# Moving three small parameter loads and their transpose behind other work, in a one-core SSM + SwiGLU kernel

## The chip, the core and the metric

The kernel runs on one core of a Trainium2 chip. The core has four compute engines with queues of their own: TensorE (PE in the profile; PEld is its weight load), VectorE (DVE), ScalarE (ACT) and GpSimd (POOL). SyncE (SP) only issues transfers. Each engine takes its instructions in the order of its queue, and engines wait for each other by semaphores. Transfers can be issued from SyncE's, ScalarE's and GpSimd's queue; all of them are carried out by the core's 16 DMA engines. Matrix products land in PSUM, which has eight banks; everything else lies in SBUF.

The metric is device time in microseconds (us), the median over several executions. A profile is one further execution, with every instruction's start and duration. Its times count from the first instruction, so its span is a little shorter than the device time of the same execution.

## The reference

The input x has 2048 tokens of 512 features. It is normalised, and then two branches run on the result and are added to x: an S5 state-space layer (A) and a SwiGLU feed-forward layer (B).

```
xn = layernorm(x)
# A: S5, state size 512, complex
dt = exp(log_dt);  Lam = Lambda_re + 1j * Lambda_im
Lam_bar = exp(dt * Lam)
Bu = xn @ (((Lam_bar - 1) / Lam)[:, None] * (B_re + 1j * B_im)).T
h[t] = Lam_bar * h[t - 1] + Bu[t]
y = 2 * Re(h @ C.T) + xn * Dskip
# B: SwiGLU, hidden size 1376
ffn = (silu(xn @ w_gate) * (xn @ w_up)) @ w_down
out = x + y + ffn
```

The change concerns the three vectors Lambda_re, Lambda_im and log_dt, of 512 bf16 numbers (1 KB) each.

## The kernel before

The 2048 tokens are cut into 16 token tiles of 128, and these into 4 chunks of 512. For chunks 1 to 3 the normalised tokens are transposed by DMA, and gate, up, B's projection and the output products run on the transposed chunk. The first chunk is treated in another way, so that TensorE has work before all of x and all statistics are there: token tiles 0 to 3 are transposed on TensorE (`raw_mm`, `cT_mm`, line 244), their mean is taken off, and gate and up of each tile are multiplied with the centred tile (`head_mm`, `sw_mm`, line 488) while the factor 1/std is applied when the products are read out of PSUM (`sw_out`, lines 497 and 498). Weights of gate and up come in three groups (`wg0`, `wu0`; `wg1`, `wu1`; `w_end`).

The order of each engine's queue is the order of the program text: the schedule is written by hand (`tc.manual_schedule()`), and the tail of the function is that order. Later work on VectorE is queued in a backlog and let out by an estimate of TensorE's time (`pump`, `need`).

What bears on the change:

- **The parameter vectors.** `prm_rows` is a tile of 128 by 128, set to zero on GpSimd (line 141). Three loads on GpSimd's queue (line 143) put each vector into four of its rows. These stand near the beginning of GpSimd's queue. `prm_transpose` (lines 278 to 281) transposes the tile on TensorE into bank `p1` (line 280), and VectorE copies the 12 useful columns to `prm` (line 281). TensorE's weight load for it waits for all three loads.
- **dt and what follows.** `exp_pool` raises e to the power on GpSimd (line 284): `dt_t` from `prm`, later `r_t`. `params_a` (lines 287 to 289) and `params_sin` (lines 325 to 341) follow on VectorE and ScalarE; ScalarE's two sines stand between its `sw_out` of token tile 1 and that of token tile 2. The tables (line 300 and on) take `ws2` and `jidx`.
- **Around it on GpSimd.** Four powers for 1/std of token tiles 1, 0, 3 and 2 (line 197); `pad_last` (lines 510 and 512) and an iota for `jidx` (line 725).
- **Around it on VectorE.** The copies of the transposed token tile 1 (line 256), statistics (lines 187 to 196), centring (line 234), and `norm_dve` (line 205), which normalises token tiles 0 to 3 for the DMA transpose of chunk 0 (`xT_dma(0)`, line 264, SyncE's queue).
- **PSUM.** Eight banks are handed round in the order in which they come free; a matmul into a bank waits for the last reader of what was there.
- **SyncE's queue at that time** issues, in this order: the second group of gate and up, `w_end` for gate and up (line 114), token tiles 4 to 7 of x (line 144), the DMA transpose of B_re (line 148), and then `xT_dma(0)`.

In the order written by hand, the stretch around the transpose is:

```
    head_mm(0, 2)
    for k in range(KD):
        cT_mm(p0, xc[:, 3, :], k, k == 0, k == KD - 1)
    cT_copy(nc.scalar.copy, p0, 3)
    prm_transpose()
    exp_pool(dt_t[:], ldt)
    pad_last()
```

Of the kernel before, what the change touches and what calls it, by code (L numbers as in the profile page):

```python
# [23 lines left out]
def kernel(  # L24
# [17 lines left out]
    nc = tc.nc  # L42
# [10 lines left out]
    NQ = Pst // 128  # L53
# [20 lines left out]
    def bank(shape=(128, CW), dtype=F32):  # L74
        return psum.tile(list(shape), dtype, name="ps")
# [62 lines left out]
    load_w1(nc.sync, wg_g, wg_v, 2)  # L138
    load_w1(nc.sync, wu_g, wu_v, 2)
    prm_rows = const.tile([128, 128], BF16, name="prm_rows")  # L140
    nc.gpsimd.memset(prm_rows[:], 0.0)
    for i, v in enumerate((A_Lambda_re, A_Lambda_im, A_log_dt)):
        nc.gpsimd.dma_start(out=prm_rows[i * NQ:(i + 1) * NQ, :], in_=v.rearrange("(q j) -> q j", j=128))
    nc.sync.dma_start(out=xall[:, TPC:2 * TPC, :], in_=x_v[:, TPC:2 * TPC, :])

    def load_bt(part):
# [31 lines left out]
    def xn_tile(c):  # L178
        if c not in xn_c:
            xn_c[c] = lnp.tile([128, KD, TPC, 128], BF16, name="xn")  # L180
        return xn_c[c]

    def by_k(ap):
        return ap.rearrange("p (k d) -> p k d", d=128)

    def ln_stats(n):
        nc.vector.bn_stats(out=stats[:, n, 0, :], in_=xall[:, n, :])  # L187
        nc.vector.bn_aggr(out=mv[:, n, :], in_=stats[:, n, 0, :])
# [14 lines left out]
    def norm_dve(n):  # L203
        c, i = divmod(n, TPC)
        nc.vector.tensor_scalar(out=xn_tile(c)[:, :, i, :], in0=by_k(xall[:, n, :]), scalar1=mv[:, n, 0:1],
                                scalar2=rstd[:, n:n + 1], op0=ALU.subtract, op1=ALU.mult)
# [19 lines left out]
    def mean_act(i):  # L226
        nc.scalar.activation(out=xnT[:, NCH - 1, 0, :], in_=xall[:, i, :], func=ACT.Copy, scale=1.0 / D,
                             accum_out=mean2[:])
# [26 lines left out]
    def cT_copy(copy, ps, i, k0=0, k1=KD):  # L255
        copy(out=xcT[:, k0:k1, i * 128:(i + 1) * 128], in_=by_k(ps[:, k0 * 128:k1 * 128]))  # L256
# [6 lines left out]
    def xT_dma(c):  # L263
        nc.sync.dma_start_transpose(out=runs(xnT[:, c]), in_=xn_tile(c)[:].rearrange("p k i d -> p (k i d)"))

    prm = const.tile([128, 3, NQ], F32, name="prm")
    lre, lim, ldt = prm[:, 0, :], prm[:, 1, :], prm[:, 2, :]

    def sm(name, *shape):
        return const.tile([128, *shape], F32, name=name)  # L270

    dt_t, r_t, dre = sm("dt_t", NQ), sm("r_t", NQ), sm("dre", NQ)
# [5 lines left out]
    def prm_transpose():  # L278
        pp = p1[:, 0:128]
        nc.tensor.matmul(pp, lhsT=prm_rows[:], rhs=ident[:], start=True, stop=True)  # L280
        V.tensor_copy(out=prm[:].rearrange("p t q -> p (t q)"), in_=pp[:, 0:3 * NQ])

    def exp_pool(out, in_):
        nc.gpsimd.tensor_tensor(out=out, in0=e_t[:], in1=in_, op=ALU.pow)
# [200 lines left out]
    def sw_mm(ps, groups, gi, i, k0=0, k1=KD):  # L485
        a, b = fgroups[gi]
        for k in range(k0, k1):
            nc.tensor.matmul(ps[:, 0:(b - a) * 128], lhsT=xcT[:, k, i * 128:(i + 1) * 128], rhs=groups[gi][:, k, 0:(b - a) * 128],  # L488
                             start=(k == 0), stop=(k == KD - 1))
# [19 lines left out]
    def pad_last():  # L509
        nc.gpsimd.memset(g0[:, FT - 1, :, FR:128], 0.0)  # L510
        for t in g_last:
            nc.gpsimd.memset(t[:, :, FR:128], 0.0)
# [157 lines left out]
    def head_mm(which, i, k0=0, k1=KD):  # L670
        if held[i][which] is None:
            held[i][which] = bank()
        sw_mm(held[i][which], (G, U)[which], 0, i, k0, k1)
# [22 lines left out]
    for k in range(HK, KD):  # L696
        for i in range(2):
            head_mm(0, i, k, k + 1)
    ln_stats(1)
    mean_act(2)  # L700
    ln_rstd(1, 2)
# [17 lines left out]
    for k in range(KD):  # L719
        cT_mm(p0, xc[:, 3, :], k, k == 0, k == KD - 1)  # L720
    cT_copy(nc.scalar.copy, p0, 3)
    prm_transpose()
    exp_pool(dt_t[:], ldt)
    pad_last()
    nc.gpsimd.iota(out=jidx[:], pattern=[[1, CW]], base=0, channel_multiplier=0,
                   allow_small_or_imprecise_dtypes=True)
    sw_out(0, 0, *held[0])
    head_mm(1, 2)
    for n in range(TPC):
        norm_dve(n)  # L730
    xT_dma(0)
    params_a()
# [146 lines left out]
```

## Time and profile before

| | us |
|---|---|
| median of 3 runs (lowest, highest) | 178.70 (178.49, 178.71) |
| the profiled execution's own time | 178.46 |
| its span, first to last instruction | 176.4 |
| TensorE busy | 172.9 (98% of the span) |
| VectorE busy | 158.1 (90%) |
| ScalarE busy | 106.6 (60%) |
| GpSimd busy | 27.8 (16%) |

The granted TensorE clock is 0.999. The page's rows of busy tenths cut the span into 40 slices of 4.4 us each; the DMA row gives the mean busy share of the 16 DMA engines:

```profile
PE   8999999999999999999999999999999999999993
DVE  3899999999999999999999999999999997799133
POOL 5272300050000000047000000024100002416100
DMA  6999839999996000037015000007410000993712
```

A 9 is 90% or more. TensorE is busy from the first slice to the last but one. VectorE has hardly a gap until slice 33. GpSimd works little, most of it in the first slices. The DMA engines are filled in slices 1 to 3 (4 to 18 us), where x, the weights and B's matrices come in.

In the profile's lists, a line of the timeline gives start, duration, engine, program line, operation, output <- inputs, and count; square brackets give the idle time before it and what ended it. "us to landing" is the time from the issue of a transfer to its completion. A group such as "x4" is four instructions in a row; matmuls overlap, so a group's duration is a little longer than the distance to the next one's start.

### The profile page before, as it was taken

The numbers are of one execution on the slowest core, as the hardware profiler recorded it, in microseconds if no ns is written. First come the engines' busy times: TensorE is split into PE (matmuls) and PEld (weight loads), VectorE is DVE, ScalarE is ACT, GpSimd is POOL, SyncE is SP. The second block draws the span as 40 slices with busy tenths as digits, with TensorE's granted clock in tenths as the row PEclk, the third lists the DMA queues.
The fourth block names the chain that finished last, engine by engine and source line by source line (L and its number), as shares of the span: only waits on it lengthen the run. The fifth ranks groups of instructions, "written<-read, shape, count | busy, mean of one in ns | idle before, by whom it ended". The sixth has DMA issues, their size and how long they took to land.

```text
span 176.4 us, 2469 instructions
## 1 busy us (share of the span) xinstructions
PE 172.9 (98%) x904; PEld 85.4 (48%) x904; DVE 158.1 (90%) x261; ACT 106.6 (60%) x192; POOL 27.8 (16%) x39
## 2 busy tenths in 40 slices
PE   8999999999999999999999999999999999999993
PEld 4444755564444444446444444446444444444743
DVE  3899999999999999999999999999999997799133
ACT  4468989978976687036896661024666657962000
POOL 5272300050000000047000000024100002416100
PEclk9999999999999999999999999999999999999999
DMA  6999839999996000037015000007410000993712
GB/s 169 340 351 203 177 88 250 224 169 337 238 238 238 4 0 0 0 33 85 16 20 119 0 0 0 0 4 71 48 30 2 4 0 0 160 181 48 90 44 75
DMA packets 35179, 17.88 MB, mean 101 GB/s; under 512 B 25008, under 2 KB 35088, under 8 KB 35120
## 3 DMA queue, kind: packets, MB, share of 16 engines
q1 hardware_dynamic: 30992, 13.96, 33.8%
q0 software_dynamic: 3456, 3.28, 14.6%
q10 hardware_dynamic: 720, 0.49, 0.9%
q8 instruction: 7, 0.11, 0.3%
q14 instruction: 4, 0.03, 0.1%
HBM read 8.03 MB, written 5.24 MB: 75 GB/s over the span
## 4 chain that ended last, share of the span: by engine, by line
PE 97%; DMA 1%; DVE 0%; issue 0%
PE ps L461 29%; PE ps L579 22%; PE ps L589 16%; PE ps L386 16%; PE ps L488 10%; PE ps L521 3%; DMA xall<-in_A_x_dram 1%; PE ps L244 1%; PE ps L252 0%; DVE xall L592 0%; PE ps L646 0%; PE ps L280 0%
## 5 line engine op out<-in xcount | busy, mean ns | idle before, releaser
L579 PE MATMUL ps<-wd_sb,guT 128*128 128x512 bf16 (+3 forms) x198 | 38.8, 355 | 0.0
L428 DVE TENSOR_TENSOR_SCAN g<-r_t,car,u 128x512 bf16<-128x512 f32 x24 | 29.1, 1264 | 0.0
L589 PE MATMUL ps<-CF,wt 128*128 128x512 bf16 (+2 forms) x144 | 28.3, 355 | 0.0
L386 PE MATMUL ps<-xnT,BT 128*128 128x512 bf16 x128 | 28.3, 379 | 0.0
L579 PEld LDWEIGHTS <-guT 128*128 128x128 bf16 (+1 forms) x198 | 18.5, 98 | 19.9
L461 PE MATMUL ps<-xnT,wg 128*128 128x512 bf16 x96 | 24.6, 379 | 0.0
L461 PE MATMUL ps<-xnT,wu 128*128 128x512 bf16 x96 | 24.6, 379 | 0.0
L596 POOL DMA_DIRECT2D out_dram<-res x12 | 10.5, 1043 | 81.6 <-ACT res L595 76.0
L595 ACT CAST res<-ps 128x512 bf16<-128x512 f32 x12 | 7.0, 584 | 24.7 <-PE ps L589 24.7
L388 ACT CAST u<-ps 128x512 bf16<-128x512 f32 x32 | 18.2, 590 | 5.9 <-PE ps L386 5.8
L475 ACT ACTIVATE guT<-ps 128x512 bf16<-128x512 f32 x30 | 17.9, 596 | 6.1 <-PE ps L461 6.1
L476 ACT CAST u<-ps 128x512 bf16<-128x512 f32 x30 | 17.6, 587 | 6.0 <-PE ps L461 6.0
L589 PEld LDWEIGHTS <-wt 128*128 128x128 bf16 x144 | 13.4, 98 | 14.3
L386 PEld LDWEIGHTS <-BT 128*128 128x128 bf16 x128 | 12.5, 98 | 14.7
L551 ACT ACTIVATE xr<-xall,nb,rstd 128x512 bf16<-128x512 bf16 x16 | 11.8, 804 | 5.2 <-DVE xall L559 3.0
L461 PEld LDWEIGHTS <-wu 128*128 128x128 bf16 x96 | 9.4, 98 | 11.3
L461 PEld LDWEIGHTS <-wg 128*128 128x128 bf16 x96 | 9.4, 98 | 10.6
L488 PEld LDWEIGHTS <-CF 128*128 128x128 bf16 x96 | 9.1, 98 | 8.0 <-ACT CF L256 0.8
L197 POOL TENSOR_TENSOR rstd<-ve,neg_half 128x1 f32<-128x1 f32 (+1 forms) x7 | 7.6, 1084 | 26.7 <-DVE ve L196 26.7
L461 PE MATMUL ps<-xnT,w_end 128*128 128x512 bf16 x48 | 10.8, 379 | 0.0
L187 DVE BATCH_NORM_STATS2 stats<-xall 128x6 f32<-128x512 bf16 x15 | 10.1, 674 | 0.2 <-DMA xall<-in_A_x_dram 0.2
L480 DVE TENSOR_TENSOR guT<-guT,u 128x1024 bf16<-128x1024 bf16 x15 | 10.0, 675 | 0.0
(120 smaller groups left out, 217.9 us busy)
## 6 DMA issues: line engine op xcount, KB each, us to landing
out_dram<-in_A_x_dram SPq DMA_DIRECT2D x3, 512.0 KB, 5.2
out_dram<-res POOLq DMA_DIRECT2D x12, 128.0 KB, 3.1
out_dram<-xall POOLq DMA_DIRECT2D x3, 512.0 KB, 6.1
wd_sb<-in_B_w_down_dram SPq DMA_DIRECT2D x1, 1280.0 KB, 7.2
xall<-in_A_x_dram SPq DMA_DIRECT2D x1, 1024.0 KB, 7.3
wu<-in_B_w_up_dram SPq DMA_DIRECT2D x2, 256.0 KB, 4.4
wg<-in_B_w_gate_dram SPq DMA_DIRECT2D x1, 512.0 KB, 5.3
wu<-in_B_w_up_dram SPq DMA_DIRECT2D x1, 512.0 KB, 5.4
```

The source lines that it names most:

```text
L187: nc.vector.bn_stats(out=stats[:, n, 0, :], in_=xall[:, n, :])
L386: nc.tensor.matmul(ps[:], lhsT=BT[:, part, k, q * 128:(q + 1) * 128], rhs=xnT[:, c, k, :], start=(k == 0), stop=(k == KD - 1))
L388: nc.scalar.copy(out=u_tiles[c][:, part, q, :], in_=ps[:])
L428: V.tensor_tensor_scan(out=g()[:, part, q, :], data0=r_t[:, q:q + 1].to_broadcast([128, CW]), data1=u_tiles[c][:, part, q, :], initial=ini ...
L461: nc.tensor.matmul(ps[:fs, lo:hi], lhsT=wslice(groups, fi, k), rhs=xnT[:, c, k, lo:hi], start=(k == 0), stop=(k == KD - 1))
L475: nc.scalar.activation(out=guT[:fs, fi, :], in_=psg[:fs], func=ACT.Silu)
L476: nc.scalar.copy(out=u_pair[c][:fs, fi % 2, :], in_=psu[:fs])
L488: nc.tensor.matmul(ps[:, 0:(b - a) * 128], lhsT=xcT[:, k, i * 128:(i + 1) * 128], rhs=groups[gi][:, k, 0:(b - a) * 128], start=(k == 0), s ...
L551: nc.scalar.activation(out=box["xr"][:], in_=xall[:, n, :], func=ACT.Identity, scale=rstd[:, n:n + 1], bias=nb[:, n:n + 1])
L579: nc.tensor.matmul(o[:], lhsT=gu_tiles[c][:fsz[fi], fi, i * 128:(i + 1) * 128], rhs=wd_sb[:fsz[fi], fi, lo:hi], start=(fi == 0), stop=False)
L589: nc.tensor.matmul(o[:], lhsT=w_tiles[c][:, part, q, i * 128:(i + 1) * 128], rhs=CF[:, part, q, lo:hi], start=False, stop=(part == 1 and q ...
L596: nc.gpsimd.dma_start(out=out_v[:, n, lo:hi], in_=res[:, lo:hi], accum_op=ALU.add)
```

## The change

The memset of `prm_rows` and its three loads become a function, `load_prm`, called behind the copies of token tile 1 instead of near the start. The memset is done by VectorE instead of GpSimd; the loads stay on GpSimd's queue. The transpose and the power for `dt` move from behind the copy of token tile 3 into the loop that normalises token tiles 0 to 3, ahead of the third of them.

```
@@ -138,9 +138,12 @@
     prm_rows = const.tile([128, 128], BF16, name="prm_rows")
-    nc.gpsimd.memset(prm_rows[:], 0.0)
-    for i, v in enumerate((A_Lambda_re, A_Lambda_im, A_log_dt)):
-        nc.gpsimd.dma_start(out=prm_rows[i * NQ:(i + 1) * NQ, :], in_=v.rearrange("(q j) -> q j", j=128))
+
+    def load_prm():
+        nc.vector.memset(prm_rows[:], 0.0)
+        for i, v in enumerate((A_Lambda_re, A_Lambda_im, A_log_dt)):
+            nc.gpsimd.dma_start(out=prm_rows[i * NQ:(i + 1) * NQ, :], in_=v.rearrange("(q j) -> q j", j=128))
+
@@ -696,6 +699,7 @@
     for k in range(HK, KD):
         for i in range(2):
             head_mm(0, i, k, k + 1)
+    load_prm()
     ln_stats(1)
     mean_act(2)
@@ -719,14 +723,15 @@
     cT_copy(nc.scalar.copy, p0, 3)
-    prm_transpose()
-    exp_pool(dt_t[:], ldt)
     pad_last()
     nc.gpsimd.iota(out=jidx[:], pattern=[[1, CW]], base=0, channel_multiplier=0,
                    allow_small_or_imprecise_dtypes=True)
     sw_out(0, 0, *held[0])
     head_mm(1, 2)
     for n in range(TPC):
+        if n == 2:
+            prm_transpose()
+            exp_pool(dt_t[:], ldt)
         norm_dve(n)
     xT_dma(0)
```

In the built program this gives, queue by queue: on TensorE the transpose stands behind the four matmuls of up of token tile 2 and ahead of gate of token tile 3; on VectorE the memset stands between the copy of token tile 1 and its statistics, and the copy of `prm` between the second and the third `norm_dve`; on GpSimd the three issues stand ahead of the four powers for 1/std, and the power for `dt` behind `pad_last` and the iota. The number of instructions is the same. SyncE's and ScalarE's queues keep their order. Since `p1` now comes free later, banks are handed round a little differently: up of token tile 3 takes the bank that held gate of token tile 0, and the first matmul group with the second group of weights takes `p1`.

More of the change, by code (lines that the diff above doesn't have):

```diff
@@ L140, with load_prm @@
     prm_rows = const.tile([128, 128], BF16, name="prm_rows")
-    nc.gpsimd.memset(prm_rows[:], 0.0)
-    for i, v in enumerate((A_Lambda_re, A_Lambda_im, A_log_dt)):
-        nc.gpsimd.dma_start(out=prm_rows[i * NQ:(i + 1) * NQ, :], in_=v.rearrange("(q j) -> q j", j=128))
+    def load_prm():
+        nc.vector.memset(prm_rows[:], 0.0)
+        for i, v in enumerate((A_Lambda_re, A_Lambda_im, A_log_dt)):
+            nc.gpsimd.dma_start(out=prm_rows[i * NQ:(i + 1) * NQ, :], in_=v.rearrange("(q j) -> q j", j=128))
     nc.sync.dma_start(out=xall[:, TPC:2 * TPC, :], in_=x_v[:, TPC:2 * TPC, :])
@@ L698 @@
             head_mm(0, i, k, k + 1)
+    load_prm()
     ln_stats(1)
@@ L721 @@
     cT_copy(nc.scalar.copy, p0, 3)
-    prm_transpose()
-    exp_pool(dt_t[:], ldt)
     pad_last()
@@ L729 @@
     for n in range(TPC):
+        if n == 2:
+            prm_transpose()
+            exp_pool(dt_t[:], ldt)
         norm_dve(n)
```

## The prediction

> **What bounds the kernel now.** I read the chain of work that ended last first, then TensorE's waits, then the order of time on each engine around the moved lines, and last the transfers in flight there. The page's chain line and the one wait that TensorE has:
>
> ```profile
> PE 97%; DMA 1%; DVE 0%; issue 0%
> ```
> ```profile
> PE ps L646 <- PEq L863: 0.8, 1, 0.8
> ```
>
> After its first instruction TensorE (PE) waits for nobody that the profile shows until its last matmul at 173.7. So whatever holds its queue up is added to the time one for one, and nothing gets faster by being relieved elsewhere. A speeded-up VectorE or ScalarE is worth nothing here. TensorE around the transpose (start, duration, line):
>
> ```profile
> 9.79 0.39 PE L244 MATMUL ps<-ident,CF 128*128 128x128 bf16 x4
> 10.01 0.22 PE L280 MATMUL ps<-ident,prm_rows 128*128 128x128 bf16 x1
> 10.07 1.03 PE L488 MATMUL ps<-wu,CF 128*128 128x512 bf16 x4
> 10.93 1.03 PE L488 MATMUL ps<-wg,CF 128*128 128x512 bf16 x4
> ```
>
> L280 takes a slot of 0.06 (10.07 - 10.01). Behind the four matmuls of up of token tile 2 it would start at 10.93 - 0.06 = 10.87. That is the due time of the parameter rows after the change, against 10.01 before: 0.86 later. GpSimd (POOL) before:
>
> ```profile
> 1.78 0.71 POOL L143 DMA_DIRECT2D prm_rows<-in_A_Lambda_re_dram  x1 [0.31 <-POOL prm_rows L141]
> 2.48 0.56 POOL L143 DMA_DIRECT2D prm_rows<-in_A_Lambda_im_dram  x1
> 3.03 0.52 POOL L143 DMA_DIRECT2D prm_rows<-in_A_log_dt_dram  x1
> ...
> 11.26 1.02 POOL L284 TENSOR_TENSOR dt_t<-e_t,prm 128x4 f32<-128x4 f32 x1
> 12.23 0.20 POOL L510 MEMSET guT<- 128x128 bf16 x1
> ```
>
> The third load is issued at 3.03. What the reader is to see next is how long a load is under way while the weights fill the DMA engines (issues in narrow windows: size, us from issue to landing):
>
> ```profile
> xall<-in_A_x_dram SPq DMA_DIRECT2D x1, 128.0 KB, 4.3
> prm_rows<-in_A_Lambda_im_dram POOLq DMA_DIRECT2D x1, 1.0 KB, 3.9
> wu<-in_B_w_up_dram SPq DMA_DIRECT2D x1, 256.0 KB, 4.3
> prm_rows<-in_A_log_dt_dram POOLq DMA_DIRECT2D x1, 1.0 KB, 4.1
> ```
> ```profile
> w_end<-in_B_w_gate_dram SPq DMA_DIRECT2D x1, 352.0 KB, 5.6
> w_end<-in_B_w_up_dram SPq DMA_DIRECT2D x1, 352.0 KB, 6.2
> xall<-in_A_x_dram SPq DMA_DIRECT2D x1, 512.0 KB, 7.0
> ```
> ```profile
> dsk_bc<-in_A_Dskip_dram POOLq DMA_DIRECT2D x1, 128.0 KB, 5.8
> wd_sb<-in_B_w_down_dram SPq DMA_DIRECT2D x1, 96.0 KB, 7.2
> ```
>
> With the issue times of the SyncE and GpSimd timelines: xall tile 2 (2.13) lands at 6.4, Lambda_im (2.48) at 6.4; wu's first half (2.60) at 6.9, log_dt (3.03) at 7.1. A load of 1 KB on GpSimd's queue lands together with the large transfer that SyncE issued just before it. Much later it is the same: dsk_bc (38.63) lands at 44.4, the 96 KB of wd_sb issued at 37.33 at 44.5. So the small loads stand behind the backlog that is there when they are issued, and that backlog grows: w_end gate, issued at 6.44, lands at 12.0; w_end up (6.86) at 13.1; xall tiles 4 to 7 (7.52) at 14.5.
>
> **The change part by part.**
>
> *Memset.* GpSimd's memset of 0.21 goes; VectorE does one of the same tile, behind the copies of token tile 1. Nearest rows: 0.17 for minus_mean's memset of the same size, 0.06 for one of four columns. I take 0.1 to 0.17. VectorE comes to it at about 5.5 (L187 starts at 5.52 before). The 0.33 that it idles before L234 at 7.27 takes this up. Without that idle, 0.15 would reach the copy of token tile 2 and TensorE's four L244 behind it.
>
> *The three issues.* GpSimd waits for the memset (done at about 5.65) and then starts the first issue 0.3 later, as at L143 before (0.31 idle): 5.95. With the spacings of before (0.70 and 0.55) the others start at 6.65 and 7.2, the last ends at 7.72. Queued behind them on GpSimd is the power for rstd of tile 1 (6.69 before, now about 7.75 to 8.35). Its readers are ScalarE at 11.85 and VectorE at 11.1, and the next one on GpSimd waits for VectorE until 8.47 anyway: nothing on the path. SyncE's queue is not touched. The 96 small packets leave the window of 4 to 7 us; the wu half that TensorE takes at 6.98 may land a few hundredths earlier, but TensorE is then busy, so no gain.
>
> *Landing, the disputed term.* Not shown before: a GpSimd load issued at 7.2 into this backlog. Bounds: the shortest transfers of GpSimd's queue, out_dram<-res with a median of 3.1 in the page's list of issues, give 10.3; the transfer issued next after it, xall at 14.5, is the other end. Between them, by neighbours in issue time (two pairs within 0.2, and dsk_bc within 0.1), log_dt at 7.2 belongs to w_end up at 6.86: 13.1. log_dt landed 0.2 behind its neighbour before, Lambda_im level with it. I take 13.2.
>
> *TensorE.* L280's weight load waits for all three loads, and TensorE's queue is in order. It starts at 13.25 instead of 10.87: 2.4 idle. Behind it stand gate and up of token tile 3 and then the rest. A stop costs some 0.05 more where a weight load is no longer hidden (0.10 each), less 0 for the slot itself, which only moves. So +2.4 on the path, bounds 0 (landing at 10.3) and 3.7 (landing at 14.5).
>
> *What is late next.* VectorE's copy of prm (L281) now stands between the second and third normalisation. VectorE finishes two of them at about 11.4 (0.38 each), waits to 13.5, and ends the fourth at 14.4. The transpose of token tiles 0 to 3 (L264) waits for that; SyncE's queue was busy with B's transpose until 14.31 and issued it at 14.43, so 0.1 at most, for a use at 22.95 that itself moves by 2.4. The power for dt, now behind pad_last and the iota (1.0 together, 12.23 to 13.24 before, now about 11.4 to 12.4), starts with the copy at 13.7 and takes 1.02; VectorE's chain from L287 starts at 14.75 instead of 12.31, the sine on ScalarE at 15.95 instead of 13.50. That is 2.45, TensorE's own shift. ScalarE's evacuation stays as far behind TensorE as it was, and PSUM banks come free in time: the tightest, the one read at 14.10 to 14.77 and written again at 16.11, keeps its 1.3. Later consumers (B's results at 73, the scans) keep their distance to TensorE in the same way.
>
> Sum against the profiled execution: span 176.4 + 2.4 = 178.8, and 2.06 lie around it (178.46 - 176.4): 180.9. The median shown is 178.7, 0.24 above that execution, so **181.1** for the median.
>
> **The rivals.**
>
> *One turn each.* The DMA engines let the small load go in turn with the large transfers rather than behind all of them. Three loads then pass one large transfer each: behind wg's second group (issued 4.15, 5.3 to landing: 9.4), wu's (5.49 + 5.4: 10.9) and w_end gate (12.0). Landing 12.0, idle 1.2, time 179.9. For it: the three loads before landed 0.5 and 0.7 apart, as turns would. Against it: dsk_bc had no turn inside the 1280 KB of wd_sb that ran before it. [...]
>
> *Its own latency, hence not slower.* What counts is GpSimd's own way of issuing, and the 3.9 to 4.1 are mostly that. Then a load issued at 7.2 lands at 11.2 (idle 0.4, 179.1) or, with the 3.1 of out_dram<-res, at 10.3, before 10.87, and TensorE never waits. Left is that dt's power goes behind the iota: VectorE and ScalarE fall back by 1.05, less than the 1.3 that the bank at 16.11 has, so the time is 178.7. It decides from a latency under 3.65. For it: the 3.1 rows; against: they ran while hardly anything else moved.
>
> *One place further back, or a slow clock.* If the three issues take longer than before, log_dt falls behind xall at 14.5: idle 3.7, 182.4. Or the pause slows TensorE: the first matmuls of 512 columns run 0.43 apart against 0.216 later, for about 4.3 us from the start, though the clock row shows 9; that again would cost up to 2.1, 183.2. [...]
>
> **How the numbers follow.** Forecast (landing 12.7 to 13.6, 180.6 to 181.5): 0.58. One turn each (179.4 to 180.4): 0.20. Own latency with a small wait (about 179.1): 0.06; with none (178.7): 0.07. Further back or slow clock (182.4 and up): 0.07. Something that none of these names: 0.02. About 0.2% (0.36) is what can be told from no change. Faster needs TensorE to lose idle time that it doesn't have; I leave it that last 0.02 and 0.01 of the no-wait case. Within 0.2%: the rest of the no-wait case and a third of the small wait, 0.08. Slower: 0.89. The range 179.1 to 182.2 holds the first two cases, their edges and most of the small wait; some 0.15 are left out.
>
> **What would show it.** A TensorE wait before the transpose, released by DMA of prm_rows, near 2.4, with the three issues at 5.9 to 7.7 and "to landing" near 6 instead of 4. The normalisation of tiles 2 and 3 behind it. Wrong if prm_rows lands within 4, if L281's copy comes at 11.5, if TensorE idles anywhere else (a bank, a weight), or if matmuls after the pause run 0.43 apart.

## Result and profile after

| | before | after |
|---|---|---|
| median, us (lowest, highest) | 178.70 (178.49, 178.81) | 179.97 (179.70, 180.25) |
| profiled execution's own time | 178.46 | 180.08 |
| its span | 176.4 | 178.0 |
| start of the parameter transpose | 10.01 | 12.45 |
| mean granted clock | 0.999 | 1.000 |

The ratio is 1.0073, with a 95% interval of 1.0062 to 1.0083: the changed kernel is slower by 1.27 us, where 2.4 were predicted. The busy tenths of the page, in the rows that were shown of before:

```profile
PE   8989999999999999999999999999999999999993
DVE  3778999999999999999999999999999997799133
POOL 1564200041000000036100000014100002416100
DMA  5999919999996000026125000006310000994712
```

One digit of TensorE (PE) has changed, the 8 in the third slice (8.9 to 13.4 us); VectorE (DVE) is less busy in slices 2 to 4, and GpSimd (POOL) has moved work from the first and third slices to the second and fourth. The chain of work that ended last has a transfer in it now:

```profile
PE 93%; DMA 3%; issue 1%; POOL 1%; DVE 0%
```

The same chain in order of time (start, duration, what) says which one, and what led to it:

```profile
5.00 0.42 DVE CF L259
5.42 0.09 DVE prm_rows L143
5.51 0.30 issue
5.81 1.24 POOL prm_rows L145 x2
7.05 5.26 DMA prm_rows<-in_A_log_dt_dram
12.31 0.14 issue
12.45 0.22 PE ps L283
12.66 12.13 PE ps L491 x72
```

It is read from the top: VectorE's copies of token tile 1, its memset, the first two issues on GpSimd, the third load for 5.26 us, the transpose, and from there TensorE alone. (Line numbers are 3 higher than before from `load_prm` on, and up to 5 higher in the tail of the function.) TensorE's waits:

```profile
PE ps L283 <- DMA prm_rows<-in_A_log_dt_dram: 0.8, 1, 0.8
PE ps L649 <- PEq L868: 0.8, 1, 0.8
PE ps L491 <- DMA wg<-in_B_w_gate_dram: 0.2, 1, 0.2
```

The first is new and is the predicted one. The list puts it at 0.8, from the modelled end of the last matmul. Measured by starts it is a little more, as the timeline shows (start, duration, engine, line, operation):

```profile
5.38 0.11 DVE L143 MEMSET prm_rows<- 128x64 uint32 x1
...
5.81 0.70 POOL L145 DMA_DIRECT2D prm_rows<-in_A_Lambda_re_dram  x1 [4.49 <-DVE prm_rows L143]
...
7.05 0.52 POOL L145 DMA_DIRECT2D prm_rows<-in_A_log_dt_dram  x1
...
8.89 6.26 SPq L151 DMA_TRANSPOSE BT<-in_A_B_re_dram  x1
...
10.59 1.03 PE L491 MATMUL ps<-wu,CF 128*128 128x512 bf16 x3
...
12.45 0.22 PE L283 MATMUL ps<-ident,prm_rows 128*128 128x128 bf16 x1 [0.83 <-DMA prm_rows<-in_A_log_dt_dram]
...
12.50 1.02 PE L491 MATMUL ps<-wg,CF 128*128 128x512 bf16 x4
...
12.77 0.17 DVE L284 COPY prm<-ps 128x12 f32<-128x12 f32 x1 [1.09 <-PE ps L283]
...
13.02 1.11 POOL L287 TENSOR_TENSOR dt_t<-e_t,prm 128x4 f32<-128x4 f32 x1 [0.30 <-DVE prm L284]
...
15.07 0.21 ACT L342 ACTIVATE sin<-fs 128x8 f32<-128x8 f32 x1 [1.37 <-DVE fs L328]
...
15.27 2.16 SPq L267 DMA_TRANSPOSE xnT<-CF  x1
```

Up of token tile 2 starts at 10.59 and its four matmuls take 0.86 to the next start, so the transpose was due at 11.45. It starts at 12.45: 1.0 lost. The gate of token tile 3 starts at 12.50 against 10.93 before, 1.57 later. Of this, 1.0 is the wait, and 0.58 was there already: up of token tile 2 should have started at 10.01 without the transpose's slot in front, and started at 10.59. This execution had got its weights later (the wait of 0.2 at L491 is part of that). The experiments below show whether that belongs to the change.

Nothing is lost or gained after that. The sine is at 15.07 against 13.50, and VectorE's last addition, which ends the core's work, at 175.32 against 173.75: 1.57 both times.

### The profile page after: what moved, and what is told of

The parts are those of the page before. It is cut to its first block, busy times and chain, and to the rows that moved or that the text cites. A ratio compares the mean times of both kernels' runs of the same rounds, so it can differ in the third digit from the quotient of the medians.

```text
span 178.0 us, 2453 instructions
## 1 busy us (share of the span) xinstructions
PE 172.6 (97%) x888; PEld 85.5 (48%) x904; DVE 157.8 (89%) x262; ACT 106.7 (60%) x192; POOL 27.6 (16%) x38
## 4 chain that ended last, share of the span: by engine, by line
PE 93%; DMA 3%; issue 1%; POOL 1%; DVE 0%
PE ps L464 29%; PE ps L582 21%; PE ps L592 15%; PE ps L389 15%; PE ps L491 7%; PE ps L524 3%; DMA prm_rows<-in_A_log_dt_dram 3%; PE ps L649 1%; POOL prm_rows L145 1%; PE ps L247 1%; PE ps L255 0%; DVE CF L259 0%; DVE xall L595 0%; PE ps L283 0%; DVE prm_rows L143 0%
## 5 line engine op out<-in xcount | busy, mean ns | idle before, releaser
L582 PE MATMUL ps<-wd_sb,guT 128*128 128x512 bf16 (+4 forms) x197 | 38.7, 355 | 0.1
L582 PEld LDWEIGHTS <-guT 128*128 128x128 bf16 (+1 forms) x198 | 18.5, 98 | 19.9
L599 POOL DMA_DIRECT2D out_dram<-res x12 | 10.5, 1043 | 82.1 <-ACT res L598 76.6
L592 PEld LDWEIGHTS <-wt 128*128 128x128 bf16 x144 | 13.4, 98 | 14.3
L464 PEld LDWEIGHTS <-wg 128*128 128x128 bf16 x96 | 9.4, 98 | 10.6
L491 PEld LDWEIGHTS <-CF 128*128 128x128 bf16 x96 | 9.2, 98 | 8.3 <-ACT CF L259 1.1
L190 DVE BATCH_NORM_STATS2 stats<-xall 128x6 f32<-128x512 bf16 x15 | 10.1, 670 | 0.0
```

The costliest lines, as they stand in the source:

```text
L464: nc.tensor.matmul(ps[:fs, lo:hi], lhsT=wslice(groups, fi, k), rhs=xnT[:, c, k, lo:hi], start=(k == 0), stop=(k == KD - 1))
L582: nc.tensor.matmul(o[:], lhsT=gu_tiles[c][:fsz[fi], fi, i * 128:(i + 1) * 128], rhs=wd_sb[:fsz[fi], fi, lo:hi], start=(fi == 0), stop=False)
L592: nc.tensor.matmul(o[:], lhsT=w_tiles[c][:, part, q, i * 128:(i + 1) * 128], rhs=CF[:, part, q, lo:hi], start=False, stop=(part == 1 and q ...
L599: nc.gpsimd.dma_start(out=out_v[:, n, lo:hi], in_=res[:, lo:hi], accum_op=ALU.add)
```

## The experiments

All edits but the fifth are against the changed kernel. Each ratio is against the kernel before on the same chip. "Starts" below means the start of the parameter transpose in the profiled execution.

**1. The new order with the loads early.** Memset (GpSimd) and loads go back to the start of GpSimd's queue; the transpose stays where the change puts it.

```
     prm_rows = const.tile([128, 128], BF16, name="prm_rows")
-    def load_prm():
-        nc.vector.memset(prm_rows[:], 0.0)
-        for i, v in enumerate((A_Lambda_re, A_Lambda_im, A_log_dt)):
-            nc.gpsimd.dma_start(out=prm_rows[i * NQ:(i + 1) * NQ, :], in_=v.rearrange("(q j) -> q j", j=128))
+    nc.gpsimd.memset(prm_rows[:], 0.0)
+    for i, v in enumerate((A_Lambda_re, A_Lambda_im, A_log_dt)):
+        nc.gpsimd.dma_start(out=prm_rows[i * NQ:(i + 1) * NQ, :], in_=v.rearrange("(q j) -> q j", j=128))
...
-    load_prm()
```

> The changed kernel with the memset and the three loads back at the start of GpSimd's queue; the transpose and the power for dt stay where the change puts them. Theory A (the whole loss is TensorE waiting for parameter rows that are issued into a backlog of weights): rows landed by about 7.1, no TensorE wait at the transpose, VectorE's chain from dre on about 1 us later than before and absorbed; time 178.7, within 0.2 of before. Rival B (the loss, or half of it, comes from the new order on VectorE, GpSimd and ScalarE, or from banks handed round differently): 179.3 or more, with a TensorE wait on ScalarE or VectorE near 16 us.

Measured: 178.68, ratio 0.9989 (0.9972 to 1.0007). TensorE's waits and the transpose on the timeline of this run:

```profile
PE ps L646 <- PEq L864: 0.8, 1, 0.8
PE ps L488 <- DMA wu<-in_B_w_up_dram: 0.2, 1, 0.2
```
```profile
11.10 0.22 PE L280 MATMUL ps<-ident,prm_rows 128*128 128x128 bf16 x1
```

No square bracket: the transpose didn't wait. The moved transpose, the other order of banks and the later power for dt (12.80 here, 11.26 before) cost nothing that can be measured. The loss is in the loads, or in the memset that went back with them; experiment 3 has that memset on VectorE and loses nothing.

**2. The loads late with the transpose in its old place.**

```
     cT_copy(nc.scalar.copy, p0, 3)
+    prm_transpose()
+    exp_pool(dt_t[:], ldt)
...
     for n in range(TPC):
-        if n == 2:
-            prm_transpose()
-            exp_pool(dt_t[:], ldt)
         norm_dve(n)
```

> Loads late as in the change, transpose and power for dt back ahead of up of token tile 2. Theory A: the rows land at the same time (about 12.3) and the transpose is due 0.86 earlier, so TensorE waits 1.9 instead of 1.06 and the time is 0.9 above the changed kernel: 180.8. If the loads' own latency from the issue were what counts (4 us), the wait would be about 1.0: 179.7. Rival B: no more than the changed kernel's 180.0.

Measured: 180.80, ratio 1.0111 (1.0087 to 1.0136). The timeline:

```profile
12.85 0.22 PE L283 MATMUL ps<-ident,prm_rows 128*128 128x128 bf16 x1 [2.80 <-DMA prm_rows<-in_A_log_dt_dram]
12.91 1.02 PE L491 MATMUL ps<-wu,CF 128*128 128x512 bf16 x3
```

The transpose, due four matmuls earlier, waits 2.8 where 1.9 were expected. `log_dt`, issued at 7.19, landed at 12.7, 0.4 later than in the changed kernel's profile, and TensorE came to the transpose at 10.05, some 0.5 earlier than it would have there. The ratio is 0.4% (0.68 us) above that of the changed kernel, near the 0.86 of those four matmuls. The second line matters for the clock: after a pause of 2.8 us the group takes 1.02 (three of its four records are there) and the next one starts 0.86 later, as without a pause.

**3. The loads late with the transpose later still**, behind up of token tile 3, the sines moved along.

```
     for n in range(TPC):
-        if n == 2:
-            prm_transpose()
-            exp_pool(dt_t[:], ldt)
         norm_dve(n)
     xT_dma(0)
-    params_a()
...
     head_mm(1, 3)
-    params_sin()
+    prm_transpose()
+    exp_pool(dt_t[:], ldt)
+    params_a()
...
                 sw_out(0, 3, *held[3])
+                params_sin()
```

> Loads late as in the change, the transpose, the power for dt and params_a behind up of token tile 3, params_sin behind the read-out of token tile 3, so that TensorE is due at the transpose at about 13.0. Theory A: the rows land at 12.3 to 13, the wait is gone and the time is 178.7 to 179.0. If in addition the early weights really come later because the loads were moved (wg's third row block landed at 6.47 in the changed kernel's profile against 5.51 before, TensorE 0.5 late by 8 us), that stays: 179.2. Rival B: still 179.5 or more, as the chain behind dt is later yet.

Measured: 178.71, ratio 0.9998 (0.9983 to 1.0012). TensorE's only wait, and the transpose on the timeline:

```profile
PE ps L649 <- PEq L867: 0.8, 1, 0.8
```
```profile
12.78 0.22 PE L283 MATMUL ps<-ident,prm_rows 128*128 128x128 bf16 x1
```

The loads are as late as in the changed kernel (issued at 5.74, 6.43 and 7.06; the last lands 4.8 later, at 11.9), and nothing is lost. So the whole loss is TensorE's wait, and neither the memset on VectorE nor the issues ahead of GpSimd's powers cost anything. The 0.58 of the profile above is not the change's either.

**4. One load late instead of three.** Memset and the first two loads early on GpSimd, `log_dt` alone behind the power for rstd of token tile 1.

```
+    nc.gpsimd.memset(prm_rows[:], 0.0)
...
+    load_prm(0)
+    load_prm(1)
...
-    load_prm()
     ln_stats(1)
     mean_act(2)
     ln_rstd(1, 2)
+    load_prm(2)
```

> Lambda_re and Lambda_im loaded at the start, log_dt alone on GpSimd's queue behind the power for token tile 1, so issued at about 7.3; transpose where the change puts it. Behind the backlog (the load lands with the large transfer that SyncE issued just before it, w_end up): 13.1 or later, 5.8 or more to landing, TensorE waits 2.2 or more, 181. One turn each (a single load lets one large transfer go): landing by 10.9, no wait, 178.7. Own latency (4.1 from the issue): landing 11.4, wait 0.5, 179.2.

Measured: 179.74, ratio 1.0059 (1.0040 to 1.0078). The timeline, and the transfers issued from 5.9 to 7.1 (size, us from issue to landing):

```profile
6.99 0.56 POOL L145 DMA_DIRECT2D prm_rows<-in_A_log_dt_dram  x1
...
12.23 0.22 PE L285 MATMUL ps<-ident,prm_rows 128*128 128x128 bf16 x1 [1.21 <-DMA prm_rows<-in_A_log_dt_dram]
```
```profile
w_end<-in_B_w_gate_dram SPq DMA_DIRECT2D x1, 352.0 KB, 6.4
w_end<-in_B_w_up_dram SPq DMA_DIRECT2D x1, 352.0 KB, 6.9
prm_rows<-in_A_log_dt_dram POOLq DMA_DIRECT2D x1, 1.0 KB, 5.1
```

None of the three landings expected came. `log_dt` lands at 12.1. That is before both parts of `w_end` (issued by SyncE at 5.90 and 6.41, landed at 12.3 and 13.3), though it was issued after them, so it does not stand behind the whole backlog. It is also 1.2 later than by one turn. And it is as late alone (12.1) as the third of three is (11.9 to 12.7 in the changed kernel and experiments 2 and 3): how many loads there are does not matter, when the last is issued does.

**5. Small loads as probes.** The kernel before, with five further 1 KB loads of `log_dt` on GpSimd's queue into a tile that nothing reads.

```
+    def probe(i):
+        nc.gpsimd.dma_start(out=probe_rows[i * NQ:(i + 1) * NQ, :], in_=A_log_dt.rearrange("(q j) -> q j", j=128))
...
             ln_rstd(c * TPC, (c + 1) * TPC)
+            if c == 1:
+                probe(3)
+                probe(4)
...
     ln_rstd(1, 2)
+    probe(0)
...
     ln_rstd(0, 1)
+    probe(1)
...
     params_a()
+    probe(2)
```

> The kernel before with five extra loads of log_dt (1 KB) into a scratch tile on GpSimd's queue: behind the powers for token tiles 1 and 0 (issued about 7.3 and 9.1), behind the power for r_t (about 14.3) and two behind the power for token tiles 4 to 7 (about 21 to 22). Nothing reads them; only their times to landing count. Behind the whole backlog: 6 to 7 us for the first and about 8 for the second (with B's transpose, issued at 8.3 and landing at 17.1). A wait of bounded depth (the engines hold only some 2.5 us of work ahead of a newcomer): 5 to 5.5 for both, and about 3 for the last two, when hardly anything moves. Own latency: 4 for all.

Measured in a single execution: 178.74. The loads by issue (size, us to landing): at 7.14, at 9.05, at 14.27, at 20.99, and the median of that and the last one, at 21.5, together:

```profile
probe_rows<-in_A_log_dt_dram POOLq DMA_DIRECT2D x1, 1.0 KB, 5.0
...
probe_rows<-in_A_log_dt_dram POOLq DMA_DIRECT2D x1, 1.0 KB, 6.0
...
probe_rows<-in_A_log_dt_dram POOLq DMA_DIRECT2D x1, 1.0 KB, 4.2
...
probe_rows<-in_A_log_dt_dram POOLq DMA_DIRECT2D x1, 1.0 KB, 1.7
...
probe_rows<-in_A_log_dt_dram POOLq DMA_DIRECT2D x2, 1.0 KB, 1.6
```

None of the three lists that were expected came whole. The bounded depth that the second list rests on was my estimate; no run shows it. The last two loads take 1.7 and 1.6, of which the issue is half a microsecond. The DMA engines were still full when the first of these two was issued, but they ran empty by 22.0, and the packets of both (the single pieces that the profile counts in the engines, 32 for each of these loads) move between 22 and 23. So such a load takes 1.6 to 1.7 where its packets meet empty engines, and the rest of the 4 to 6 us of the others is waiting.

The first three don't wait for the same thing. The first lands at 12.1, ahead of `w_end` up (issued at 6.88, landed at 13.4). The second lands at 15.1, level with x (8.05, landed at 15.0), and the third at 18.5, close behind B's transpose (8.62, landed at 18.3): these two did land together with a large transfer issued before them. The packets show the difference. None of the first load's move before 10.5, and all have moved by 11.7; it waits ahead of its packets. The third's all move between 15.9 and 16.5, within 2.3 of its issue, and it is complete only 2 us after them.

**6. The one late load on ScalarE's queue**, as in 4 but issued at 5.57 behind ScalarE's copy of token tile 1.

```
+    nc.gpsimd.memset(prm_rows[:], 0.0)
...
+    load_prm(0, nc.gpsimd)
+    load_prm(1, nc.gpsimd)
...
-    load_prm()
+    load_prm(2, nc.scalar)
     ln_stats(1)
```

> Lambda_re and Lambda_im loaded at the start, log_dt alone on ScalarE's queue behind its copy of token tile 1 (issue at 6.0 to 6.5, which may push ScalarE's mean of token tile 2 back by up to 0.4). If the wait lies in the DMA engines, it lands 5 or more after the issue, near 11.5, and TensorE waits 0.5 to 1.0: 179.2 to 179.7. If it lies in GpSimd's way of issuing: 4 or less, landing by 10.5, no wait at the transpose: 178.7 to 179.0.

Measured: 179.30 (178.49 to 179.44), ratio 1.0031 (1.0016 to 1.0046). The profiled execution is the fastest of them, and its transpose (at 10.71) does not wait. The profile gives no time to landing for that load, but it has its packets: between 5.2 and 14, ScalarE's queue moves eight packets, all between 8.8 and 9.8, which is 3.2 to 4.2 after the issue. TensorE's weight load for the transpose, which needs them, starts at 10.49, so the load landed by then, at most 4.9 after its issue. A load issued at 5.47 on GpSimd's queue (experiment 7) took 4.6. So in this execution the wait is not particular to GpSimd's way of issuing. Neither case came as expected: the issue was earlier, at 5.57 instead of 6.0 to 6.5. Why the other nine executions took 178.9 to 179.4 no profile shows.

**7. The three loads 1.6 us earlier**, behind VectorE's diagonal for token tile 0.

```
     diag_dve(0)
+    load_prm()
...
-    load_prm()
```

> The changed kernel with load_prm behind the first diag instead of behind the copies of token tile 1: the memset at about 4.2, the third issue at about 5.8 instead of 7.05. Theory A: landing at 10.7 to 11.1, TensorE waits 0 to 0.3 at the transpose, time 178.7 to 179.0, so about 1 of the 1.3 us comes back. Rival (the number of loads or the new order costs, not their time): 179.5 or more.

Measured: 178.88, ratio 1.0010 (0.9996 to 1.0025). The third issue and the transpose:

```profile
5.47 0.52 POOL L145 DMA_DIRECT2D prm_rows<-in_A_log_dt_dram  x1
...
10.61 0.22 PE L283 MATMUL ps<-ident,prm_rows 128*128 128x128 bf16 x1
```

`log_dt` lands 4.6 after its issue, at 10.1 (10.7 to 11.1 was expected), before TensorE comes to it. An issue 1.6 earlier gets back 1.1 of the 1.27.

**The runs together.** For each profiled execution, its time less the start of the transpose:

| kernel | time | starts | difference | TensorE waited for the loads |
|---|---|---|---|---|
| before | 178.46 | 10.01 | 167.59 (with the 0.86 of up taken off) | no |
| 1, loads early | 178.69 | 11.10 | 167.59 | no |
| 7, loads 1.6 earlier | 178.11 | 10.61 | 167.50 | no |
| 4, one load late | 179.82 | 12.23 | 167.59 | 1.2 |
| after | 180.08 | 12.45 | 167.63 | 0.8 |
| 6, one late on ScalarE's queue | 178.49 | 10.71 | 167.78 | not in this execution |
| 5, probes | 178.74 | 10.12 | 167.76 (with the 0.86 of up taken off) | no |
| 2, transpose early | 181.20 | 12.85 | 167.49 (with the 0.86 of up taken off) | 2.8 |

In "before", 2 and 5 the transpose stands ahead of up of token tile 2, hence the 0.86. (Experiment 3 has it elsewhere and is left out.) The difference is the same to 0.3, and without experiments 5 and 6 to 0.14, while the time moves over 3.1. So what follows the transpose takes the same time in all of them, and the start of the transpose decides the time. Without a wait that start varies from 10.6 to 11.1 between executions; the two latest arrivals of TensorE, in the changed kernel and in experiment 1, go with a wait of 0.2 for weights. With a wait it is the landing. For the medians this gives a start of 178.70 - 167.59 = 11.1 before (as if behind up) and 179.97 - 167.6 = 12.4 after.

## Why the prediction was right or wrong

**What bounds the kernel, and what a wait of TensorE costs: right.** One for one, as the table shows.

**Memset and issues: right.** The memset took 0.11 and was absorbed (experiment 3 has it and loses nothing). The issues came at 5.81, 6.50 and 7.05, where 5.95, 6.65 and 7.2 were predicted. The powers for rstd behind them cost nothing.

**The landing: the term that was mis-sized.** "Log_dt at 7.2 belongs to w_end up at 6.86: 13.1 ... I take 13.2." It landed at 12.3, 5.3 after its issue instead of 6.0. The rule behind it, "a load of 1 KB on GpSimd's queue lands together with the large transfer that SyncE issued just before it", had been read from two pairs issued at 2.1 to 3.0, where each waited about 4, and from a 128 KB load at 38.6. It was carried over to a place where SyncE's own transfers wait 6 to 7, and there it doesn't hold. The transfers of the changed kernel issued from 6.4 to 7.5:

```profile
wu<-in_B_w_up_dram SPq DMA_DIRECT2D x1, 512.0 KB, 5.5
w_end<-in_B_w_gate_dram SPq DMA_DIRECT2D x1, 352.0 KB, 6.1
w_end<-in_B_w_up_dram SPq DMA_DIRECT2D x1, 352.0 KB, 6.6
...
prm_rows<-in_A_log_dt_dram POOLq DMA_DIRECT2D x1, 1.0 KB, 5.3
```

SyncE issued `wu` at 6.44 and the halves of `w_end` at 6.86 and 7.41, so they land at 11.9, 13.0 and 14.0. `log_dt`, issued at 7.05, should by the rule have landed with the first half, at 13.0, and landed at 12.3. It overtook a transfer issued before it, here as in experiment 4. The rule does not always fail: the second and third loads of experiment 5 did land level with a large transfer issued before them. (SyncE's issue times scatter between executions: `wu` went out at 5.2 to 5.9 in the other eight traces, with the loads early or late.)

**The sum: the median's distance was added once too often.** I added 0.24 because the median lay that far above the profiled execution. A later start of TensorE is swallowed by the wait, since the landing decides when it ends. By the table the start was put at 13.25 + 0.24 = 13.5 and was 12.4: 1.1 too much, of which 0.24 is this and 0.9 the landing. That is the whole distance between 181.1 and 179.97. (That the landing itself doesn't move with TensorE's delay between executions is taken for granted here; no run separates the two.)

The time came outside the window of the case that was forecast, 180.6 to 181.5, and inside that of *One turn each*, 179.4 to 180.4. That it lies in the stated range is owed to the range holding both.

**What is late next: right in effect.** Sine and chain are late by TensorE's own shift, and no bank is waited for. The DMA transpose of token tiles 0 to 3 was held to 15.27 by B's transpose ahead of it on SyncE's queue (8.89 + 6.26 = 15.15), not by VectorE, and cost nothing.

**The rivals.** *Its own latency* is half right: where its packets meet empty DMA engines a load takes 1.6 to 1.7, lower than the 3.1 that I took from the stores, but here it doesn't meet empty engines. *A slow clock* falls: after a pause of 2.8 (experiment 2) the group of up takes 1.02 and the next one starts 0.86 later, as without a pause. No run here shows a longer one. *One turn each* gave 179.9, the number that came, for a reason that the runs don't support: three turns for three loads would have let the single load of experiment 4 land by 10.9, and it landed at 12.1. That it landed ahead of two transfers issued before it (12.3 and 13.3) agrees with turns of some kind; how the engines share their time between transfers, and how long a turn is, no run shows.

**What stays open** is why it takes 5 us. The runs show that it is waiting (1.6 to 1.7 on empty engines against 4.2 to 6.0 into the backlog), that it isn't the whole backlog (4), that it doesn't depend on the number of small loads (4), and that a load on ScalarE's queue waits as well (6). In experiment 4 most of it passes before the load's first packet moves: of the 32 packets none moves between the issue at 6.99 and 10.6, all move by 11.7, and the load lands at 12.1. On empty engines (5) the first packet moves about 1.1 after the issue. What holds the first packet back, and what held the completion of the third load of experiment 5 when its packets were through, was not settled.

No version here beats the kernel before. Experiments 1, 3 and 7 are level with it, and the trace of the kernel before shows no wait of TensorE, behind its first instruction, that could be won.

## What to carry to other kernels

Price a moved load by its landing against the time at which the bounding engine comes to it, not by the microseconds that its issue moved: here an issue 4 us later cost 1.27, one 2.4 us later nothing that could be measured, and one as late with its reader 1.7 us further back nothing either. Take the time from issue to landing from loads of the same size that were issued into a like backlog of transfers (that the engines are full at the moment of the issue is not enough: one such load took 1.7); where the trace has none, add one that nobody reads and take its time. And where the bounding engine waits for a landing, delays of that engine ahead of the wait do not add to it, provided that they leave the landing where it is, which no run here tests.

## What the runs showed of the hardware that was not expected

- A 1 KB load on GpSimd's queue took 1.6 to 1.7 us from issue to landing where its packets met empty DMA engines (experiment 5), and 3.5 to 6.0 in all nine traces while x, the weights and B's matrix were coming in.
- Such a load overtook 352 KB transfers that SyncE had issued 0.2 to 1.1 us before it: 12.3 against 13.0 in the changed kernel, 12.1 against 12.3 and 13.3 in experiment 4. Others landed level with a large transfer issued before them: 15.1 and 15.0, 18.5 and 18.3 in experiment 5, and 44.4 and 44.5 for the 128 KB load behind `wd_sb` in the kernel before.
- In experiment 4 a load's first packet moved some 3.7 us after its issue; in experiment 5 another's packets had all moved within 2.3 us, and it was complete 2 us later.
- On ScalarE's queue a 1 KB load issued at 5.57 moved its packets 3.2 to 4.2 us later (experiment 6).
- TensorE's matmuls of 512 columns kept their 1.02 a group of four after pauses of 1.0 and 2.8 us.
